# State updates cut into 64x64 products, and three moves in the order of a chunked retention prologue

## The chip, the cores and the metric

The kernel runs on one core of a Trainium2 chip. The core has TensorE (PE, with its weight loads shown apart as PEld), VectorE (DVE), ScalarE (ACT) and GpSimd (POOL), each with its own instruction stream, and SyncE (SP), whose queue issues the DMAs here. The metric is device microseconds of one execution, as the median over runs. A profiled execution has a span besides, from the first to the last instruction; its own time is a little longer than that.

## The reference, cut to what matters

Inputs are q, k and v of 4 batches, 8 heads, 768 positions and 64 columns, and three weight matrices of a bilinear FFN. The first part is a recurrence over the positions, the second a product over all 3072 tokens.

```python
gamma = 1.0 - 2.0 ** (-5.0 - np.arange(H))
for t in range(S):
    state = gamma * state + k[t] (outer) v[t]        # 64x64 for each batch and head
    y[:, :, t] = q[t] @ state / sqrt(64)
x = y, heads side by side                            # 3072 x 512
out = ((x @ w_a) * (x @ w_b)) @ w_out                # 512 -> 1536 -> 512
```

## The kernel before

Powers of gamma are folded into k and q when these are scaled, so the state is a plain running sum of k-by-v products. Positions are worked in slots of 128, two slots to a pair, and each slot in two chunks of 64 (c = 0 and 1). Within a chunk, a score matrix is formed (`scores`), masked to the causal part (`mask`), and multiplied by v (`intra`); what comes from earlier chunks is q times the state (`inter`). Both are summed in PSUM as y, and copied to xt, the FFN's input. The FFN makes a and g for 12 column blocks of 128 (`ffn_a`, `ffn_g`), multiplies them into ht, and forms the output rows (`ffn_out`).

The first batch, three pairs of slots (u = 0, 1, 2), has its own functions with a 2 in their names. For these a pair is loaded with even and odd positions apart (par = 0 and 1). For pairs 0 and 1:

- `casts2` (line 376) scales k and q and casts v, on DVE or POOL as the caller says; `scaled` is line 212, the casts are line 184.
- `flip2` (line 387) transposes k or q on TensorE (line 396) and copies the result out on ACT (line 182) as kT and qT.
- `scores2` (line 399) makes the scores of one parity (line 409) in PSUM, `mask2` (line 415) multiplies them by the mask on DVE (line 420), in two halves of rows.
- `update2` (line 423) adds a chunk's k-by-v products to the state in the PSUM tile st (line 432): for each parity and each of four head pairs one matmul with a contraction of 64 positions, 128 columns of k as weights and 128 columns of v. The product is 128x128, of which the two 64x64 blocks on the diagonal are used. `keep_state` (line 439) copies those blocks, a half of the partitions each, into the bf16 tile gbd, of which there are two, one for each chunk.
- `intra2` (line 455, matmul at 465) and `inter2` (line 444, matmul at 450) make y; `inter2` reads gbd[0] for c = 0 and gbd[1] for c = 1. `leave2` (line 470) copies y to xt, one chunk on each of two engines.
- `warm` (line 485) runs matmuls on zeros whose result nobody reads.

The order on each engine is the order of the program: every instruction is tied to the one before it on its engine. So the list of calls from line 553 on is the order of the work, on TensorE, ACT, DVE, POOL and SP alike, and an engine does nothing else while its next instruction waits. State tile st is one buffer: an update waits for the copies of the state that still read it. The pool psff has three buffers, taken in turn by transposes, scores, a and g; y0, y1, at and st have one each.

The DMA loads are issued on SP in the order of `LOADS` (line 20): k, q of pair 0, k, q of pair 1, v of both, then weights; POOL casts the weights as they land (`cast_w`, line 186, and `cast_o`).

Of the kernel before, what the change touches and what calls it, by code (L numbers as in the profile page):

```python
# [9 lines left out]
F32 = mybir.dt.float32  # L10
# [13 lines left out]
def kernel(  # L24
# [39 lines left out]
    psat = ctx.enter_context(tc.tile_pool(name="psat", bufs=1, space=bass.MemoryType.PSUM))  # L64
    psst = ctx.enter_context(tc.tile_pool(name="psst", bufs=1, space=bass.MemoryType.PSUM))
# [110 lines left out]
    wa_bf = wpool.tile([P, KT, DFF], BF16, name="wa_bf")  # L176
# [3 lines left out]
    def cast(engine, dst, src):  # L180
        if engine is nc.scalar:
            seq(nc.scalar.copy(dst, src))  # L182
        else:
            seq(engine.tensor_copy(dst, src))  # L184
# [50 lines left out]
    def half(i):  # L235
        return slice(64 * i, 64 * i + 64)
# [178 lines left out]
    def mask2(u, par, rows=(0, 1)):  # L415
        t = 2 * u + par
        if t not in aT:
            aT[t] = tra.tile([P, 2, HP, P], BF16, tag="aT", name="aT")
        for r in rows:
            seq(nc.vector.tensor_tensor(aT[t][:, r], ats[t][r], masks[par].to_broadcast([P, HP, P]),  # L420
                                        op=ALU.mult))

    def update2(u, c, on=(nc.scalar, nc.scalar)):
        if (u, c) == (PAIRS - 1, 1):
            return
        if (u, c) == (0, 0):
            state[0] = psst.tile([P, HP, P], F32, tag="st", name="st")
        st = state[0]
        for par in range(2):
            for hp in range(HP):  # L430
                t = 2 * u + par
                seq(nc.tensor.matmul(st[:, hp, :], kb[t][half(c), hp, :, :],  # L432
                                     vb[t].rearrange("p (r hp) d -> p hp r d", r=2)[half(c), hp],
                                     start=((u, c, hp, par) == (0, 0, 0, 0)),
                                     stop=(hp == HP - 1), skip_group_check=True))
        if on:
            keep_state(c, on)

    def keep_state(c, on=(nc.scalar, nc.scalar)):

        for r in range(2):
            cast(on[r], gbd[1 - c][half(r), :, half(r)], state[0][half(r), :, half(r)])

    def inter2(u, last=False):
        for c in range(2):
# [9 lines left out]
    def intra2(u, par, begin, home=None):  # L455
        if begin and home is None:
            ys[u] = [psat.tile([P, HP, P], F32, tag=f"y{c}", name="y") for c in range(2)]
        elif begin:
            both = psat.tile([P, 2, HP, P], F32, tag=home, name="y")
            ys[u] = [both[:, c] for c in range(2)]  # L460
        t = 2 * u + par
        for r in range(2):
            for hp in range(HP):
                for c in range(2):
                    seq(nc.tensor.matmul(ys[u][c][half(hp % 2), 2 * r + hp // 2, :],  # L465
                                         vb[t][half(c), HP * r + hp, :], aT[t][half(c), r, hp, :],
                                         start=(begin and r == 0 and hp < 2), stop=not begin,
                                         skip_group_check=True))

    def leave2(u, on):  # L470
        J, i = where[2 * u]
        if i == 0 and J not in xt:
            xt[J] = xtp.tile([P, 4, KT, P], BF16, tag="xt", name="xt")
        for c, eng in enumerate(on):
            if eng is None:
                continue
            cast(eng, xt[J][:, i + c].rearrange("p k (m par) -> p k par m", par=2),
                 ys[u][c].rearrange("p k (par m) -> p k par m", par=2))

    def xcols(J, kt, c0, c1):  # L480
        if J < 2:
            return xt[J][:, c0 // P : c1 // P, kt, :]
        return xt[J][:, kt, c0:c1]

    def warm(n, pool, tag, w=2 * P):
        idle = pool.tile([P, 4 * P], F32, tag=tag, name="idle")
        for _ in range(n):
            seq(nc.tensor.matmul(idle[:, :w], zero[:, :P], zero[:, :w], start=True, stop=True,  # L488
                                 skip_group_check=True))
# [2 lines left out]

    asbs = {}

    def ffn_a(J, ft, c0=0, c1=None):
        c1 = TILES[J] * P if c1 is None else c1
        if J not in ht:
            ht[J] = htp.tile([P, NFT, 4 * P], BF16, tag="ht", name="ht")
        fs = slice(ft * P, (ft + 1) * P)
        a = psff.tile([P, 4 * P], F32, tag="ff", name="a")[:, : c1 - c0]  # L500
        for kt in range(KT):
            seq(nc.tensor.matmul(a, wa_bf[:, kt, fs], xcols(J, kt, c0, c1),  # L502
                                 start=(kt == 0), stop=(kt == KT - 1)))
        asb = asbs[J, ft, c0] = asbp.tile([P, 4 * P], BF16, tag="asb", name="asb")[:, : c1 - c0]
        seq(nc.scalar.copy(asb, a))  # L505

    def ffn_g(J, ft, c0=0, c1=None):
        c1 = TILES[J] * P if c1 is None else c1
        fs = slice(ft * P, (ft + 1) * P)
        g = psff.tile([P, 4 * P], F32, tag="ff", name="g")[:, : c1 - c0]  # L510
        for kt in range(KT):
            seq(nc.tensor.matmul(g, wb_bf[:, kt, fs], xcols(J, kt, c0, c1),  # L512
                                 start=(kt == 0), stop=(kt == KT - 1)))
        seq(nc.vector.tensor_tensor(ht[J][:, ft, c0:c1], g, asbs.pop((J, ft, c0)), op=ALU.mult))  # L514

    def ffn_ab(J, ft):
# [40 lines left out]
    casts2(1, {(V, 0): G_, (V, 1): G_})  # L557
    cast_w(0, 2)
    flip2(0, K, [((0,), A_), ((1,), A_)])
    warm(8, psat, "y1", 64)  # L560
    flip2(0, Q, [((0,), A_)])
    warm(2, psat, "y1", P)
    flip2(0, Q, [((1,), A_)])
    warm(4, psat, "y1", 192)
    scores2(0, 0)
    scores2(0, 1, True)
    mask2(0, 0, (0,))
    casts2(1, {(Q, 1): D_})
    mask2(0, 0, (1,))
    mask2(0, 1)  # L570
    flip2(1, K, [((0, 1), A_)])
    warm(3, psst, "st", 4 * P)
    flip2(1, Q, [((1,), A_), ((0,), A_)], ("y0", "y1"))
    warm(3, psst, "st", 4 * P)
    scores2(1, 0)
    update2(0, 0)
    mask2(1, 0)
    intra2(0, 0, True)
    scores2(1, 1, True)
    mask2(1, 1)  # L580
    intra2(0, 1, False)
    leave2(0, (A_, None))
    update2(0, 1)
    inter2(0, True)
    leave2(0, (None, D_))
    intra2(1, 0, True, "at")
    update2(1, 0, (A_, D_))
    intra2(1, 1, False)
    W2 = 2 * P
    ffn_a(0, 0, 0, W2)  # L590
    inter2(1, True)
    leave2(1, (A_, D_))
    ffn_a(0, 1, 0, W2)
    update2(1, 1, None)
    issue_loads(100)
# [105 lines left out]
```

## Time and profile before

| what | value |
|---|---|
| median of 3 runs | 226.9 us (226.57 to 227.45) |
| the profiled execution's own time | 227.3 us |
| its span | 225.6 us |
| TensorE busy | 217.3 us, 2556 matmuls |
| DVE, ACT, POOL busy | 97.0, 96.3, 79.7 us |
| from HBM, to HBM | 28.31 MB, 6.29 MB |

Lines of the profile that show a group give its line in the kernel, engine, operation, the tiles written and read, shapes, and the count. In the timeline the first two numbers are the start and the length in us, from the first start to the last end of a merged group; a matmul's end lies about 0.2 us behind its start even for a narrow one, since matmuls are pipelined, so what a group takes of TensorE is read from the start of one group to the start of the next. In square brackets stands the idle time of the engine before the group and what ended it. The chain lists start, length and what the end was waiting for at that time. PEld is the weight loads, which run beside PE.

### The profile page before, as it was taken

To read this page: it belongs to the slowest core of one execution; us is meant where nothing else is said; L and a number is where in the kernel's file an instruction comes from. 1 tells how busy PE (TensorE), PEld (TensorE's weight loads), DVE (VectorE), ACT (ScalarE), POOL (GpSimd) and SP (SyncE) were. 2 spreads that over 40 slices of the span, in tenths; PEclk is the share of its full clock that TensorE was granted. 3 is DMA by queue.
4 is the path that set the end of the run, shared out by engine and by line. 5 is a ranking of instruction groups with operands and counts; after the bars stand their busy time and mean duration, and the time that the engine had idled before them with its cause. 6 is when DMAs were issued, how large, how long until landed. Compare 5 with 4: busy or idle time off the path is not lost.

```text
span 225.6 us, 6154 instructions
## 1 busy us (share of the span) xinstructions
PE 217.3 (96%) x2556; PEld 130.9 (58%) x2576; DVE 97.0 (43%) x196; ACT 96.3 (43%) x207; POOL 79.7 (35%) x104
## 2 busy tenths in 40 slices
PE   7799999999999999999999999999999999999994
PEld 7567445686446867875875444545444544444443
DVE  3885246643506435562466243445243422333300
ACT  3555424342427426455457433355433354333221
POOL 5467798783636151453534262350000000000000
PEclk9999999999999999999999999999999999999999
DMA  6999999999999996979899797858100012100022
GB/s 176 347 379 382 367 293 397 310 198 223 241 222 269 241 212 128 254 148 243 169 213 167 177 275 145 196 96 142 46 0 3 0 49 96 46 0 1 3 93 94
DMA packets 96124, 39.72 MB, mean 176 GB/s; under 512 B 76000, under 2 KB 91616, under 8 KB 96096
## 3 DMA queue, kind: packets, MB, share of 16 engines
q1 hardware_dynamic: 95952, 39.20, 69.4%
q8 instruction: 20, 0.33, 0.6%
q10 hardware_dynamic: 144, 0.13, 0.2%
q14 instruction: 8, 0.07, 0.1%
HBM read 28.31 MB, written 6.29 MB: 153 GB/s over the span
## 4 chain that ended last, share of the span: by engine, by line
PE 92%; DMA 2%; ACT 2%; issue 1%; DVE 1%; SPq 0%; DVEq 0%
PE a L502 28%; PE g L512 28%; PE o L539 27%; DMA qf<-in_q_dram 2%; PE y L321 2%; PE at L280 1%; PE y L333 1%; PE st L257 1%; ACT qT L182 1%; PE st L432 1%; PE tp L396 1%; DVE kqb L212 1%; PE at L409 1%; PE y L465 1%; PE y L450 1%
## 5 line engine op out<-in xcount | busy, mean ns | idle before, releaser
L514 DVE TENSOR_TENSOR ht<-g,asb 128x256 bf16<-128x256 f32 (+1 forms) x98 | 53.9, 550 | 84.0 <-PE g L512 72.8
L512 PE MATMUL g<-xt,wb_bf 128*128 128x256 bf16 (+1 forms) x389 | 77.5, 322 | 0.2
L502 PE MATMUL a<-xt,wa_bf 128*128 128x256 bf16 (+1 forms) x389 | 77.3, 322 | 0.1
L505 ACT CAST asb<-a 128x256 bf16<-128x256 f32 (+1 forms) x98 | 46.3, 472 | 71.7 <-PE a L502 70.5
L539 PE MATMUL o<-wo_bf,ht 128*128 128x512 bf16 (+2 forms) x299 | 62.5, 362 | 1.4 <-issue 1.1
L502 PEld LDWEIGHTS <-wa_bf 128*128 128x128 bf16 x392 | 38.0, 98 | 25.0 <-DVE xt L184 0.4
L512 PEld LDWEIGHTS <-wb_bf 128*128 128x128 bf16 x392 | 38.1, 98 | 23.8
L539 PEld LDWEIGHTS <-ht 128*128 128x128 bf16 x312 | 28.8, 98 | 30.6
L212 POOL TENSOR_TENSOR kqb<-kf,ktab 128x512 bf16<-128x512 f32 x21 | 22.3, 1062 | 41.6 <-DMA kf<-in_k_dram 41.6
L182 ACT COPY osb<-o 128x512 f32<-128x512 f32 (+2 forms) x25 | 14.1, 564 | 33.4 <-PE o L539 24.2
L212 POOL TENSOR_TENSOR kqb<-qf,qtab 128x512 bf16<-128x512 f32 x21 | 21.8, 1042 | 0.9 <-DMA qf<-in_q_dram 0.7
L184 POOL CAST vb<-vf 128x512 bf16<-128x512 f32 x25 | 15.0, 612 | 19.9 <-DMA vf<-in_v_dram 10.9
L182 ACT CAST gst<-sums 128x256 bf16<-128x256 f32 x33 | 13.4, 405 | 6.1 <-DVE sums L271 2.8
L271 DVE TENSOR_TENSOR sums<-st,sums 128x256 f32<-128x256 f32 x30 | 12.7, 424 | 1.7
L286 DVE TENSOR_TENSOR aT<-at,mask 128x512 bf16<-128x512 f32 x18 | 11.5, 679 | 0.0
L344 ACT CAST xt<-y 128x512 bf16<-128x512 f32 x16 | 8.5, 583 | 0.0
L488 PE MATMUL idle<-zero 128*128 128x170 bf16 (+4 forms) x55 | 7.0, 291 | 1.3 <-DVE zero L126 1.3
L420 DVE TENSOR_TENSOR aT<-at,mask 128x512 bf16<-128x512 f32 x12 | 7.5, 680 | 1.1 <-PE at L409 1.1
L184 POOL CAST wa_bf<-wsta 128x1024 bf16<-128x1024 f32 (+1 forms) x7 | 6.4, 918 | 2.5 <-DMA wsta<-in_moe_w_a_dram 2.5
L184 POOL CAST wo_bf<-wsto 128x1024 bf16<-128x1024 f32 x6 | 6.2, 1040 | 2.2 <-DMA wsto<-in_moe_w_out_dram 2.2
L184 POOL CAST wb_bf<-wstb 128x1024 bf16<-128x1024 f32 (+1 forms) x7 | 6.4, 918 | 1.6 <-DMA wstb<-in_moe_w_b_dram 1.4
L298 DVE COPY lgr<-bq 128x1 f32<-128x1 f32 x4 | 0.6, 154 | 14.2 <-PE y L321 14.2
(54 smaller groups left out, 93.3 us busy)
## 6 DMA issues: line engine op xcount, KB each, us to landing
out_dram<-osb SPq DMA_DIRECT2D x23, 256.0 KB, 2.8
kf<-in_k_dram SPq DMA_DIRECT2D x18, 256.0 KB, 4.0
qf<-in_q_dram SPq DMA_DIRECT2D x18, 256.0 KB, 4.2
vf<-in_v_dram SPq DMA_DIRECT2D x18, 256.0 KB, 4.6
wsta<-in_moe_w_a_dram SPq DMA_DIRECT2D x6, 512.0 KB, 7.7
wstb<-in_moe_w_b_dram SPq DMA_DIRECT2D x6, 512.0 KB, 7.9
wsto<-in_moe_w_out_dram SPq DMA_DIRECT2D x6, 512.0 KB, 8.2
kf<-in_k_dram SPq DMA_DIRECT2D x3, 512.0 KB, 6.0
```

The costliest lines, as they stand in the source:

```text
L182: seq(nc.scalar.copy(dst, src))
L184: seq(engine.tensor_copy(dst, src))
L212: seq(eng.tensor_tensor(dst, src, tab, op=ALU.mult))
L271: seq(nc.vector.tensor_tensor(new, u[c][:, s], old, op=ALU.add))
L286: seq(nc.vector.tensor_tensor(aT[n][:, r].rearrange("p s h d -> p (s h) d"), at[:, r].rearrange("p s h d -> p (s h) d"), mask.to_broadcast ...
L344: seq(nc.scalar.copy(dst, ys[o][c]))
L420: seq(nc.vector.tensor_tensor(aT[t][:, r], ats[t][r], masks[par].to_broadcast([P, HP, P]), op=ALU.mult))
L502: seq(nc.tensor.matmul(a, wa_bf[:, kt, fs], xcols(J, kt, c0, c1), start=(kt == 0), stop=(kt == KT - 1)))
L505: seq(nc.scalar.copy(asb, a))
L512: seq(nc.tensor.matmul(g, wb_bf[:, kt, fs], xcols(J, kt, c0, c1), start=(kt == 0), stop=(kt == KT - 1)))
L514: seq(nc.vector.tensor_tensor(ht[J][:, ft, c0:c1], g, asbs.pop((J, ft, c0)), op=ALU.mult))
L539: seq(nc.tensor.matmul(o, ht[J][:, ft, i * P : (i + 1) * P], wo_bf[:, ft, c0:c1], start=(ft == 0), stop=(ft == NFT - 1)))
```

## The change

Four things change.

1. `update2` makes two matmuls in place of one: 64 columns of k and the 64 columns of v of the same head, so that only the two blocks that are used are computed. Each writes its own half of the partitions of st, which now has 64 columns per head pair instead of 128. An update has 16 matmuls and 16 weight loads, before 8 and 8. `keep_state` copies all columns of a half.
2. Order on TensorE: `update2(0, 0)` ahead of `scores2(1, 0)`, `update2(0, 1)` ahead of `intra2(0, 1)`, `update2(1, 0)` ahead of `intra2(1, 0)`, and `inter2(1)` ahead of the first `ffn_a`. With them ACT's order: the copies of the state after `update2(0, 1)` stand ahead of the copy of y to xt, and both copies after `update2(1, 0)` are on ACT, where one was on DVE.
3. Order on DVE: pair 1's second q scaling stands ahead of all masks, where it stood between the two halves of the first one.
4. Matmuls on zeros: 10 in place of 8 with 64 columns, 3 with 96 columns in place of 2 with 128, and 2 in place of 3 with 512 columns at two places. And the a and g products of column blocks 2 and 3 of the first FFN group are done in two halves of 256 columns instead of one of 512 (`parts`).

On POOL and SP the instructions and their order are the same.

```diff
@@ update2, keep_state
-            state[0] = psst.tile([P, HP, P], F32, tag="st", name="st")
+            state[0] = psst.tile([P, HP, D], F32, tag="st", name="st")
...
-                seq(nc.tensor.matmul(st[:, hp, :], kb[t][half(c), hp, :, :],
-                                     vb[t].rearrange("p (r hp) d -> p hp r d", r=2)[half(c), hp],
+                for r in range(2):
+                    t = 2 * u + par
+                    seq(nc.tensor.matmul(st[half(r), hp, :], kb[t][half(c), hp, r, :],
+                                         vb[t][half(c), HP * r + hp, :],
...
-            cast(on[r], gbd[1 - c][half(r), :, half(r)], state[0][half(r), :, half(r)])
+            cast(on[r], gbd[1 - c][half(r), :, half(r)], state[0][half(r), :, :])
@@ ffn_a (ffn_g alike)
+    def parts(J, ft, c0, c1):
+        if J == 0 and ft in (2, 3):
+            return [(c0, (c0 + c1) // 2), ((c0 + c1) // 2, c1)]
+        return [(c0, c1)]
...
-            seq(nc.tensor.matmul(a, wa_bf[:, kt, fs], xcols(J, kt, c0, c1),
-                                 start=(kt == 0), stop=(kt == KT - 1)))
+            for b0, b1 in parts(J, ft, c0, c1):
+                seq(nc.tensor.matmul(a[:, b0 - c0 : b1 - c0], wa_bf[:, kt, fs], xcols(J, kt, b0, b1),
+                                     start=(kt == 0 and b0 == c0), stop=(kt == KT - 1 and b1 == c1),
+                                     skip_group_check=True))
@@ the order
-    warm(8, psat, "y1", 64)
+    warm(10, psat, "y1", 64)
     flip2(0, Q, [((0,), A_)])
-    warm(2, psat, "y1", P)
+    warm(3, psat, "y1", 96)
     flip2(0, Q, [((1,), A_)])
     warm(4, psat, "y1", 192)
     scores2(0, 0)
     scores2(0, 1, True)
-    mask2(0, 0, (0,))
     casts2(1, {(Q, 1): D_})
-    mask2(0, 0, (1,))
+    mask2(0, 0)
     mask2(0, 1)
     flip2(1, K, [((0, 1), A_)])
-    warm(3, psst, "st", 4 * P)
+    warm(2, psst, "st", 4 * P)
     flip2(1, Q, [((1,), A_), ((0,), A_)], ("y0", "y1"))
-    warm(3, psst, "st", 4 * P)
+    warm(2, psst, "st", 4 * P)
+    update2(0, 0)
     scores2(1, 0)
-    update2(0, 0)
     mask2(1, 0)
     intra2(0, 0, True)
     scores2(1, 1, True)
     mask2(1, 1)
+    update2(0, 1)
     intra2(0, 1, False)
+    inter2(0, True)
     leave2(0, (A_, None))
-    update2(0, 1)
-    inter2(0, True)
     leave2(0, (None, D_))
+    update2(1, 0)
     intra2(1, 0, True, "at")
-    update2(1, 0, (A_, D_))
     intra2(1, 1, False)
+    inter2(1, True)
+    leave2(1, (A_, D_))
     W2 = 2 * P
     ffn_a(0, 0, 0, W2)
-    inter2(1, True)
-    leave2(1, (A_, D_))
     ffn_a(0, 1, 0, W2)
     update2(1, 1, None)
```

More of the change, by code (lines that the diff above doesn't have):

```diff
@@ L430, in update2 @@
             for hp in range(HP):
-                t = 2 * u + par
-                seq(nc.tensor.matmul(st[:, hp, :], kb[t][half(c), hp, :, :],
-                                     vb[t].rearrange("p (r hp) d -> p hp r d", r=2)[half(c), hp],
-                                     start=((u, c, hp, par) == (0, 0, 0, 0)),
-                                     stop=(hp == HP - 1), skip_group_check=True))
+                for r in range(2):
+                    t = 2 * u + par
+                    seq(nc.tensor.matmul(st[half(r), hp, :], kb[t][half(c), hp, r, :],
+                                         vb[t][half(c), HP * r + hp, :],
+                                         start=((u, c, hp, par) == (0, 0, 0, 0)),
+                                         stop=(hp == HP - 1), skip_group_check=True))
         if on:
@@ L511, in ffn_g @@
         for kt in range(KT):
-            seq(nc.tensor.matmul(g, wb_bf[:, kt, fs], xcols(J, kt, c0, c1),
-                                 start=(kt == 0), stop=(kt == KT - 1)))
+            for b0, b1 in parts(J, ft, c0, c1):
+                seq(nc.tensor.matmul(g[:, b0 - c0 : b1 - c0], wb_bf[:, kt, fs], xcols(J, kt, b0, b1),
+                                     start=(kt == 0 and b0 == c0), stop=(kt == KT - 1 and b1 == c1),
+                                     skip_group_check=True))
         seq(nc.vector.tensor_tensor(ht[J][:, ft, c0:c1], g, asbs.pop((J, ft, c0)), op=ALU.mult))
```

## The prediction

> **What bounds the kernel now.** I read the totals and the chain's shares first, then the stretches, then the chain and the rows of each engine between 7 and 20 us, where the diff acts.
>
> ```profile
> span 225.6 us, 6154 instructions
> PE 92%; DMA 2%; ACT 2%; issue 1%; DVE 1%; SPq 0%; DVEq 0%
> ```
> ```profile
> 10.00:15.00 5.00, 4.19 (x96) 2.85 (x95) 4.71 (x8) 3.21 (x6) 3.02 (x5) 1.00 1.11 368
> ...
> 20.00:25.00 5.00, 5.00 (x34) 3.15 (x33) 1.72 (x5) 2.54 (x6) 3.61 (x5) 1.00 1.09 384
> ```
>
> Columns of the stretches: length, busy time of PE, PEld, DVE, ACT and POOL, granted clock, DMA share, GB/s. TensorE carries 92% of the chain and from 20 us it is busy without a break, at a granted clock of 1.00. So a microsecond taken off the start of the first full FFN products is a microsecond off the end, as long as what they read has come by then. From 10 to 15 us DVE is busy 4.71 of 5.00 us, more than PE.
>
> ```profile
> 9.39 0.69 DVE aT L420
> 10.08 1.12 DVE kqb L212
> ...
> 11.68 1.08 ACT qT L182 x2
> ...
> 12.80 0.42 PE at L409 x16
> ...
> 14.61 0.74 ACT xt L182
> 15.36 0.27 ACT gbd L182
> ...
> 15.63 0.38 ACT gbd L182
> ...
> 16.05 0.60 PE st L432 x8
> ```
>
> This is the chain: pair 1's q scaling waits behind a mask on DVE, its transposes and copies wait for it, and scores of pair 1 begin at 12.80. Then PE runs, with one detour over ACT: the xt copy (0.74) stands ahead of two state copies that the next update waits for.
>
> **q scaled ahead of all masks.**
>
> ```profile
> 3.37 1.57 SPq L95 DMA_DIRECT2D qf<-in_q_dram  x1
> ```
> ```profile
> DMA to landing us min/median/max: 6.1/6.1/6.1
> ```
> ```profile
> 7.92 0.69 DVE L212 TENSOR_TENSOR kqb<-kf,ktab 128x512 bf16<-128x512 f32 x1
> 10.00 1.19 DVE L212 TENSOR_TENSOR kqb<-qf,qtab 128x512 bf16<-128x512 f32 x1
> ```
> ```profile
> 8.04 1.47 POOL L212 TENSOR_TENSOR kqb<-kf,ktab 128x512 bf16<-128x512 f32 x1 [3.81 <-DMA kf<-in_k_dram]
> 9.60 1.04 POOL L212 TENSOR_TENSOR kqb<-qf,qtab 128x512 bf16<-128x512 f32 x1
> 11.01 1.21 POOL L184 CAST vb<-vf 128x512 bf16<-128x512 f32 x2 [0.37 <-DMA vf<-in_v_dram]
> ```
>
> Pair 1's q lands at 3.37+6.1 = 9.47. DVE, free by then, would start its scaling at 9.5, just ahead of POOL's at 9.60. Two scalings at once hold each other up: at 7.92 DVE was first and took 0.69 while POOL's took 1.47; at 10.00 POOL was first and DVE's took 1.19. With DVE first it ends at 10.2 instead of 11.19, and POOL's moves from 10.64 to about 11.05, harmless to its v casts (11.01 to 12.22 become about 11.05 to 12.27). The price is on the masks: eight at 0.62 follow (rows below), from 10.1 on.
>
> ```profile
> 10.22 1.01 ACT L182 COPY kT<-tp 128x1024 bf16<-128x1024 bf16 x1 [1.35 <-PE tp L396]
> 13.81 0.76 ACT L182 CAST gbd<-st 64x256 bf16<-64x256 f32 x2 [1.05 <-PE st L432]
> ```
> ```profile
> 11.11 1.87 DVE L420 TENSOR_TENSOR aT<-at,mask 128x512 bf16<-128x512 f32 x3
> ```
>
> The 0.99 us is not all gained: ACT copies kT until 11.23, so the two qT copies (1.08 in the chain) run 11.26 to 12.33, not 11.68 to 12.76. What is late next is this kT copy: gain 0.43. Two of the six 128x512 warm products go, and the smaller warm runs ahead of them change from 8 to 10 and from 2x128 to 3x96 columns; all stand before a wait for a scaling or a copy, so I cost them at nothing; without that cover the three extra small products would cost under 0.15 us.
>
> **Updates as 64x64 products.**
>
> ```profile
> 12.80 0.42 PE L409 MATMUL at<-qT,kT 64*64 64x128 bf16 x16 [0.29 <-ACT qT L182]
> 13.15 0.62 PE L432 MATMUL st<-vb,kqb 64*128 64x128 bf16 x8
> 13.70 0.42 PE L465 MATMUL y<-aT,vb 64*64 64x128 bf16 x16
> 13.95 0.39 PE L409 MATMUL at<-qT,kT 64*64 64x128 bf16 x16
> 14.17 0.39 PE L465 MATMUL y<-aT,vb 64*64 64x128 bf16 x16
> ...
> 56.01 0.45 PE L257 MATMUL st<-vb,kqb 64*64 64x64 bf16 x32
> 56.28 0.49 PE L280 MATMUL at<-kqT 64*64 64x64 bf16 x32
> ```
>
> From start to start the old update takes 0.55, and the scores ahead of it 0.35, where the same scores followed by another 64x64 shape take 0.22: changing the shape costs some 0.1 on each side. The new form doubles the instructions to 16 weight loads and 16 matmuls of 64 columns. Line 257 has that very form: 32 in 0.27 us, spread over four quadrants, eight rounds. The new update uses two (one row half, both column halves), so 16 of them are eight rounds too: 0.27. Bounds: 0.27 if loads hide, 0.55 if nothing is won, and above that if they don't hide (a rival below). I take 0.27, the row of the same form.
>
> The Trainium skill, "TensorE: Matmul & The Clock Gate", Part 3, The mechanism, says that a weight load overlaps matmuls in flight only where its row group differs; all 16 of an update share one. By it every load would be exposed and the change would lose. This trace speaks against it: line 432's eight share a row half and still start within 0.55.
>
> **The new order, forward from 12.3.** Update(0,0) waits only for pair 0's v cast (12.27), so half of it is done in the shadow of the qT copies, the rest by 12.46. Then scores 0.22 to 12.68, intra 0.22 to 12.90, scores to 13.12 (the masks of pair 0 are done by 10.1+4x0.62 = 12.6). Now the state copies bind. An update's result comes 0.45−0.27 = 0.18 after its last start; ACT starts 0.04 later, its two copies take 0.76, and the next update, which overwrites what they read, starts 0.05 later. Copies 12.68 to 13.44, update(0,1) 13.49 to 13.76; copies 13.98 to 14.74, update(1,0) 14.79 to 15.06, with intra and inter of pair 0 inside the wait. PE idles there about 0.35 and 0.4 us. The xt copy follows those copies now, 14.72 to 15.47, and so the third pair of copies runs 15.4 to 16.14; the second half of inter(1) starts at 16.19 and ends, switch included, at 16.51. Pair 1's masks end at about 15.4, just ahead of intra(1,1): DVE is almost as late as ACT, but not later. Both of pair 1's state copies are ACT's now, and in the old order the one on DVE waited for ACT's anyway.
>
> ```profile
> 18.05 0.61 PE L502 MATMUL a<-xt,wa_bf 128*128 128x256 bf16 x4
> 18.59 0.62 PE L432 MATMUL st<-vb,kqb 64*128 64x128 bf16 x8
> 19.14 0.61 PE L512 MATMUL g<-xt,wb_bf 128*128 128x256 bf16 x4
> 19.72 1.03 PE L502 MATMUL a<-xt,wa_bf 128*128 128x256 bf16 x8
> ```
>
> Behind inter(1) come a, a, update(1,1), g. With 0.54, 0.44 (no switch behind it but the update's 0.1), 0.37 with switches, and 0.5: 16.51+1.9 = 18.4 for the first product on pair 1's columns, against 19.72. Its xt copies, ACT then DVE at 0.74 each, end near 18.2, so they cover. Gain at this point: 1.3 us.
>
> **Behind it.** Update(2,0) stands in the part where TensorE has no break and saves 0.55−0.27 = 0.28 (0.3 with the shorter scores ahead). The a and g products of column blocks 2 and 3 are cut from 512 to 2x256: 16 more matmuls and loads.
>
> ```profile
> 21.90 1.89 PE L502 MATMUL a<-xt,wa_bf 128*128 128x512 bf16 x8
> 23.63 1.89 PE L512 MATMUL g<-xt,wb_bf 128*128 128x512 bf16 x8
> ...
> 44.59 0.60 PE L502 MATMUL a<-xt,wa_bf 128*128 128x256 bf16 x4
> 45.03 0.60 PE L512 MATMUL g<-xt,wb_bf 128*128 128x256 bf16 x4
> ```
>
> A 512 takes (23.63−21.90)/8 = 0.216, two 256 take 2x0.44/4 = 0.22: the cut costs 16x0.002 to 0.004, under 0.1 us. No DMA, SP or POOL instruction is moved.
>
> Does the gain last? Weights and pair 2 come at times that DMA and POOL set. The tightest that I found:
>
> ```profile
> 30.91 2.04 POOL L212 TENSOR_TENSOR kqb<-qf,qtab 128x512 bf16<-128x512 f32 x2
> ```
> ```profile
> 35.30 0.78 PE L396 MATMUL tp<-ident,kqb 128*128 128x128 bf16 x8
> ```
>
> Pair 2's q is scaled by 32.95 and its transposes run at 35.30; 1.3 earlier, at 34.0, they still find it, with 1.0 to spare. I take the whole 1.3 as kept. If DMA held them up, the gain would shrink only from 2.3 us on.
>
> **The sum.** The profiled execution took 227.3 us, its span 225.6 and 1.7 around it. 1.3 + 0.3 − 0.04 = 1.6 off: span 224.0, time 225.7. That execution lies 0.4 above the median of 226.9, so against the median I predict 226.9 − 1.6 = 225.3.
>
> **Rivals.**
> 1. The narrow loads do not hide (slower). Place: all five updates, since their 16 loads share a row half.
> ```profile
> L257 PEld LDWEIGHTS <-kqb 64*64 64x64 bf16 x264 | 3.2, 109 | 0.4 <-issue 0.4
> ```
> A load of this form lasts 0.109. If each pair of quadrants pays it in turn, an update takes 0.27 + 8x0.109 = 1.14, which is 0.87 over my value: half of it on update(0,0), all of it on the other four, 3.9 us, so 226.9 − 1.6 + 3.9 = 229.2. It decides from where an update costs about 0.36 more than I take (1.6/4.5), 0.63 each. For it: no row of this trace has this form on one row half alone. Against it: line 257 hides loads that last as long, line 432 hides loads on one row half. 1 in 10. It is also what the skill's sentence on row groups would give.
> 2. The split products are no shorter (0.55 each), so the edit does not do what it says. Update(0,1) and (1,0) lose 0.28 each on the loop with ACT, (1,1) and (2,0) as much, (0,0) half of it: 1.3 of the 1.6 is gone, 226.6, no change. For it: twice the instructions. Against it: lines 257, 465 and 409 start theirs at 0.27 or less per 32 or 0.22 per 16. 15 in 100.
> 3. POOL takes the q scaling first, as at 10.00. Then DVE's ends at about 11.15, the qT copies at 12.7, and eight masks from 11.07 end at about 15.95; scores(1,1) wait for a mask until 13.6 and DVE sets the pace to intra(1,1). Inter(1) ends at 16.8, 0.3 later, gain 1.3, 225.6, still faster by 0.57%. For it: the two start within 0.1 us. Against: at 7.92 DVE was first by 0.12 from one landing that both waited for. 15 in 100.
> 4. Waits on ACT longer than 0.05 each, or pair 2's data late after all: gain 0.5 to 1.0, about 226.1, within 0.5%. 7 in 100.
>
> **How the numbers follow.** The forecast as it stands has 53 in 100, with its own range of 224.8 to 225.8 (each of the three ACT waits and the update known to some 0.1 to 0.15). 0.5%, 1.1 us, is about what a measurement of this kernel can tell from no change: the line is at 225.8. Faster: 53 plus 13 of case 3, 0.66. Same: cases 2 and 4 and the rest of 3, 0.24. Slower: 0.10. The range of 224.7 to 226.9 takes in cases 2 to 4 and leaves out the slower one and some above and below.
>
> **What would show it.** Scores of pair 1 starting at 12.4 to 12.5, with update(0,0) ahead of them (at 12.80 before); DVE's third scaling at 9.5 lasting 0.69 and POOL's second one over 1.3; each update 16 matmuls in 0.27 from start to start; two PE waits of 0.3 to 0.4 us ended by the state copies, and one in the middle of inter(1); the first product on pair 1's columns near 18.4 (19.72 before); the first product on column block 2 some 1.3 earlier than 21.90; pair 2's transposes not waiting for POOL. The prediction is wrong if an update takes over 0.5, if a mask rather than a state copy ends PE's waits, if the cut 2x256 products take more than two 512s' share, or if the 1.3 is handed back at a wait between 20 and 45 us.

## The result, and the profile after

The changed kernel takes 225.6 us (median of 5 runs, 225.39 to 226.01), the kernel before 226.97 (5 runs, 226.57 to 227.45). The ratio is 0.9941, with a 95% interval of 0.9921 to 0.996: 1.37 us less, 0.59%. The profiled execution took 225.51, its span 223.8.

The page of the changed kernel, its span and the shares of its chain:

```profile
span 223.8 us, 6287 instructions
...
PE 93%; DMA 3%; POOL 1%; ACT 1%; SPq 0%; issue 0%; DVE 0%; POOLq 0%
```

DVE's share of the chain has gone from 1% to 0% and ACT's from 2% to 1%, and POOL stands in it for 1%. The chain between 9 and 24 us of the changed kernel (start, length, what was waited for) tells why:

```profile
9.52 1.49 POOL kqb L212
...
11.06 0.40 PE tp L396 x4
11.45 0.45 PE idle L488 x2
...
11.94 0.55 PE st L433 x16
...
12.52 0.37 ACT gbd L182
...
12.91 0.38 ACT gbd L182
...
13.33 0.35 PE st L433 x11
```

POOL's half of pair 1's q is now the last to be scaled (9.52 to 11.01), where DVE's was. Behind it come transposes, zero products, the first update, and then twice the two state copies on ACT and the update that waits for them. TensorE's timeline of the changed kernel, in the same columns as before the change:

```profile
11.94 0.54 PE L433 MATMUL st<-vb,kqb 64*64 64x64 bf16 x16
12.29 0.42 PE L409 MATMUL at<-qT,kT 64*64 64x128 bf16 x16
12.52 0.42 PE L465 MATMUL y<-aT,vb 64*64 64x128 bf16 x16
...
13.33 0.35 PE L433 MATMUL st<-vb,kqb 64*64 64x64 bf16 x11 [0.17 <-ACT gbd L182]
13.48 0.25 PE L465 MATMUL y<-aT,vb 64*64 64x128 bf16 x2
13.51 0.23 PE L433 MATMUL st<-vb,kqb 64*64 64x64 bf16 x4
13.56 0.22 PE L465 MATMUL y<-aT,vb 64*64 64x128 bf16 x2
13.57 0.19 PE L433 MATMUL st<-vb,kqb 64*64 64x64 bf16 x1
...
14.60 0.38 PE L433 MATMUL st<-vb,kqb 64*64 64x64 bf16 x12 [0.20 <-ACT gbd L182]
...
16.21 1.05 PE L509 MATMUL a<-xt,wa_bf 128*128 128x256 bf16 x8
17.19 0.44 PE L433 MATMUL st<-vb,kqb 64*64 64x64 bf16 x16
17.56 0.61 PE L521 MATMUL g<-xt,wb_bf 128*128 128x256 bf16 x4
18.01 1.04 PE L509 MATMUL a<-xt,wa_bf 128*128 128x256 bf16 x8
...
20.19 1.91 PE L509 MATMUL a<-xt,wa_bf 128*128 128x256 bf16 x16
```

The scores of pair 1 start at 12.29 (12.80 before), the first product on pair 1's columns at 18.01 (19.72), the first on column block 2 at 20.19 (21.90). The 16 products of update(0,1) start between 13.33 and 13.57, and the next group runs on at 13.58, so they take 0.25 us; the 8 old ones of this update took 0.53 (14.62 to 15.15).

To compare runs I cut each profiled execution at places that all kernels have: the first scores of pair 0, the first product on pair 1's columns (called the mark from here on), the first and the last FFN output product, and the end of the span. "Mark 9.74" is short for 9.74 us from the first scores to the mark.

| stretch, us | before | changed | gain |
|---|---|---|---|
| start to first scores of pair 0 | 8.92 | 8.85 | 0.07 |
| to the mark | 10.80 | 9.16 | 1.64 |
| to the first output product | 33.60 | 33.43 | 0.17 |
| to the last output product | 168.92 | 168.68 | 0.24 |
| to the end of the span | 3.35 | 3.67 | −0.32 |
| span | 225.59 | 223.79 | 1.80 |

By the last output product 2.1 us have been gained, at the end 1.8. Something is given back, and not only in the last row. Near 112 us, in a stretch that the change does not touch, the changed kernel has a new wait; the rows are TensorE's, then DVE's:

```profile
111.66 0.60 PE L521 MATMUL g<-xt,wb_bf 128*128 128x256 bf16 x4
112.34 0.60 PE L509 MATMUL a<-xt,wa_bf 128*128 128x256 bf16 x4
```
```profile
110.62 0.42 DVE L524 TENSOR_TENSOR ht<-g,asb 128x256 bf16<-128x256 f32 x1 [0.45 <-PE g L521]
111.87 0.92 DVE L524 TENSOR_TENSOR ht<-g,asb 128x256 bf16<-128x256 f32 x2 [0.83 <-PE a L509]
```

Groups of four products follow each other at 0.44 all through this stage; here one takes 0.68. The ht product that should have run at about 111.49 starts at 111.87 and ends at 112.29, and TensorE's next a starts 0.05 later. In the trace DVE's wait for its operands had ended at 111.44. So 0.25 us goes on a DVE instruction that starts late although all it needs is there. And the last store takes longer to land. The rows are the DMA issues after 216 us, of the changed kernel and of the kernel before; the last number is us to landing:

```profile
out_dram<-osb SPq DMA_DIRECT2D x1, 128.0 KB, 2.0
```
```profile
out_dram<-osb SPq DMA_DIRECT2D x1, 128.0 KB, 1.7
```

These two, 0.25 and 0.32, are more than a quarter of what was gained ahead of them: 0.07 + 1.64 + 0.17 = 1.88, less 0.57 is 1.31, next to the 1.37 of the medians. (The 0.07 ahead of the first scores is not the change's: in the kernels below, e9_one_more_dve apart, these scores start anywhere from 8.71 to 8.99.) The profiled executions differ by 0.4 to 0.5 more because the stretch around 116 to 126 us took 10.08 before and 9.67 after; over all runs below but e9_one_more_dve it took 9.66 to 10.22 and followed no edit, so I don't count it.

### The profile page after: what moved, and what is told of

The parts are those of the page before. It is cut to its first block, busy times and chain, and to the rows that moved or that the text cites. A ratio compares the mean times of both kernels' runs of the same rounds, so it can differ in the third digit from the quotient of the medians.

```text
span 223.8 us, 6287 instructions
## 1 busy us (share of the span) xinstructions
PE 217.3 (97%) x2633; PEld 131.6 (59%) x2633; DVE 96.2 (43%) x195; ACT 96.6 (43%) x208; POOL 79.9 (36%) x104
## 3 DMA queue, kind: packets, MB, share of 16 engines
q1 hardware_dynamic: 95952, 39.20, 67.2%
## 4 chain that ended last, share of the span: by engine, by line
PE 93%; DMA 3%; POOL 1%; ACT 1%; SPq 0%; issue 0%; DVE 0%; POOLq 0%
PE o L549 28%; PE a L509 28%; PE g L521 28%; DMA kf<-in_k_dram 3%; PE y L321 1%; POOL kqb L212 1%; PE at L280 1%; PE y L333 1%; PE st L257 1%; PE st L433 1%; ACT gbd L182 1%; PE tp L396 1%; PE y L450 1%; PE y L465 1%; SPq L95 0%
## 5 line engine op out<-in xcount | busy, mean ns | idle before, releaser
L549 PE MATMUL o<-wo_bf,ht 128*128 128x512 bf16 (+2 forms) x312 | 64.4, 363 | 0.0
L509 PEld LDWEIGHTS <-wa_bf 128*128 128x128 bf16 x400 | 38.9, 98 | 24.2 <-issue 0.5
L521 PEld LDWEIGHTS <-wb_bf 128*128 128x128 bf16 x400 | 38.9, 98 | 22.9
L212 POOL TENSOR_TENSOR kqb<-qf,qtab 128x512 bf16<-128x512 f32 x21 | 22.3, 1066 | 1.1 <-DMA qf<-in_q_dram 1.0
```

What stands on the lines that cost most here:

```text
L212: seq(eng.tensor_tensor(dst, src, tab, op=ALU.mult))
L509: seq(nc.tensor.matmul(a[:, b0 - c0 : b1 - c0], wa_bf[:, kt, fs], xcols(J, kt, b0, b1), start=(kt == 0 and b0 == c0), stop=(kt == KT - 1 a ...
L521: seq(nc.tensor.matmul(g[:, b0 - c0 : b1 - c0], wb_bf[:, kt, fs], xcols(J, kt, b0, b1), start=(kt == 0 and b0 == c0), stop=(kt == KT - 1 a ...
L549: seq(nc.tensor.matmul(o, ht[J][:, ft, i * P : (i + 1) * P], wo_bf[:, ft, c0:c1], start=(ft == 0), stop=(ft == NFT - 1)))
```

## The experiments

"Before" is the kernel before, which ran beside each of them on the same chip. Ratios are to it, with a 95% interval, from 5 rounds.

### Which part of the change brings what

**e1_wide_update**: the changed kernel with the old products in the update, and with them the old state tile of 128 columns per head pair and its copies.

```diff
-                for r in range(2):
-                    t = 2 * u + par
-                    seq(nc.tensor.matmul(st[half(r), hp, :], kb[t][half(c), hp, r, :],
-                                         vb[t][half(c), HP * r + hp, :],
...
+                t = 2 * u + par
+                seq(nc.tensor.matmul(st[:, hp, :], kb[t][half(c), hp, :, :],
+                                     vb[t].rearrange("p (r hp) d -> p hp r d", r=2)[half(c), hp],
...
```

> The changed kernel with the old update (8 products of 128 columns, state tile of 128). Mark: start of the first product on pair 1's columns (19.72 before, 18.01 after). My theory: in the new order the pace is set by the loop of update, state copies on ACT and next update, so each update on it adds only its longer run (0.25 to 0.5, switches included) partly beside copies: mark near 18.5, update(2,0) 0.2 more, total 0.7 over the changed kernel, 226.3 us. Rival (the work counts in full, five times 0.28 and the switches): 1.4 to 1.9 over it, 227.0 to 227.5. Rival (the narrow products are no shorter): the same as the changed kernel, 225.6.

Measured: 226.81 us (226.29 to 227.46), ratio 0.9985 (0.9972 to 0.9998). Mark 9.74, 0.58 more than the changed kernel, and from the mark to the first output product 33.65, 0.22 more. So the narrow update is worth 0.80 in the trace, and 1.0 by the ratios. TensorE's rows of this kernel:

```profile
13.49 0.60 PE L432 MATMUL st<-vb,kqb 64*128 64x128 bf16 x8
14.02 0.42 PE L465 MATMUL y<-aT,vb 64*64 64x128 bf16 x16
```

0.53 from the update to what follows it, 0.25 in the changed kernel (13.33 to 13.58).

**e2_narrow_alone**: the kernel before with only this part changed (the same lines the other way round).

> The kernel before with the narrow update alone, all in the old order. My theory: update(0,0), (1,0), (1,1) and (2,0) become 0.3 shorter each on TensorE, but ACT's xt copy ahead of the state copies and DVE's xt copy hold part of it back: mark near 19.07 (0.65 earlier than 19.72), total 0.85 under before, 226.1 us. Rival (work counts in full): 1.4 to 1.9 under, 225.1 to 225.6, and then the order was worth nothing.

Measured: 226.34 us (226.1 to 226.94), ratio 0.9969 (0.9956 to 0.9981). The mark comes 0.52 sooner after the first scores (10.28), the first output product another 0.2. In the old order, too, the narrow products gain; they need no help of the new one.

**e3_q_alone**: the kernel before with only the q scaling ahead of all masks.

```diff
-    mask2(0, 0, (0,))
     casts2(1, {(Q, 1): D_})
-    mask2(0, 0, (1,))
+    mask2(0, 0)
```

> The kernel before with pair 1's second q scaling ahead of all masks, nothing else. My theory: DVE's scaling takes 0.69 from about 9.5, the kT copy holds the qT copies, scores of pair 1 start 0.44 earlier (12.36), and all of it arrives at the mark (19.28) and the end: 226.5 us. Rival (the masks, now later, take the place of the wait): scores earlier, mark unmoved, 226.9 us.

Measured: 226.64 us (226.27 to 227.25), ratio 0.9981 (0.9968 to 0.9993). Mark 10.32 after the first scores, 0.48 sooner.

**e4_mask_first**: the changed kernel with DVE's old order (the same three lines the other way round).

> The changed kernel with the old order on DVE (half of the first mask, then the q scaling, then the rest). My theory: the qT copies end 0.6 later (12.76), but update(0,0) is then wholly done beside them; the first state copies can't start before ACT is free, 0.25 later than 12.52; mark 0.25 later (18.26), total 225.85 us. Rival (the whole 0.4 to 0.6 comes back): 226.1 us. Rival (DVE's masks bind, which end no later in this order): 225.6 us.

Measured: 226.13 us (225.9 to 226.82), ratio 0.9957 (0.994 to 0.9974). Mark 9.49, 0.33 later than in the changed kernel, and 0.36 us more by the ratios. The intervals of the two ratios overlap, so it is the mark that shows the step and not the time.

**e5_no_cut**: the changed kernel with 512 columns at once in blocks 2 and 3.

```diff
-        if J == 0 and ft in (2, 3):
+        if False:
```

> The changed kernel without the cut of column blocks 2 and 3 into 2x256. My theory: the cut cost 0.04 us on TensorE and did nothing else: 225.55 us, no difference that can be measured; from the first product on block 2 to the one on block 4 3.45 us in place of 3.49. Rival (the cut keeps TensorE fed where a 512 would wait for a weight cast or a buffer): 0.2 to 0.5 slower and a wait in that stretch.

Measured: 225.85 us (225.62 to 226.0), ratio 0.9939 (0.9924 to 0.9955), not to be told from the changed kernel's 0.9941. From the mark to the first output product 33.39, 0.04 less: the price that was predicted.

**e6_old_order**: the kernel before with the narrow update and the q scaling ahead, in the old order of calls and with its zero products (e2 and e3 together).

> The kernel before with the narrow update and the q scaling ahead of the masks, but the old order on TensorE and ACT, the old warm products and no cut. My theory: mark near 18.6, 1.3 under before, 225.7 us, so the new order is worth about 0.5. Rival (the order is worth nothing once the other two are there): mark at 18.0 and 225.2 to 225.6 us. Rival (state copies behind the xt copy cost their whole 0.74): mark near 18.8, 225.9 us.

Measured: 225.89 us (225.77 to 226.45), ratio 0.9946 (0.9931 to 0.9962). Mark 9.79: 1.01 sooner than before, just the sum of 0.52 and 0.48. The new order of calls and the zero products, which the changed kernel has on top, bring 0.63 more at the mark (9.16) and next to nothing in the time (0.9941, where the intervals leave room for about half a us either way). What they bring is given back: this kernel has neither the wait at 112 us nor the slow last store (1.70). DVE's rows of this kernel at the same place:

```profile
111.19 0.43 DVE L514 TENSOR_TENSOR ht<-g,asb 128x256 bf16<-128x256 f32 x1 [0.45 <-PE g L512]
112.08 0.42 DVE L514 TENSOR_TENSOR ht<-g,asb 128x256 bf16<-128x256 f32 x1 [0.46 <-PE g L512]
```

**e7_old_warms**: the changed kernel with the old counts of zero products.

```diff
-    warm(10, psat, "y1", 64)
+    warm(8, psat, "y1", 64)
...
-    warm(3, psat, "y1", 96)
+    warm(2, psat, "y1", P)
...
-    warm(2, psst, "st", 4 * P)
+    warm(3, psst, "st", 4 * P)
...
-    warm(2, psst, "st", 4 * P)
+    warm(3, psst, "st", 4 * P)
```

> The changed kernel with the old counts of products on zeros. The prediction costed them at nothing. From the changed kernel's chain, which runs through two of them just ahead of update(0,0), I expect now: the third product of the first 512 block hidden by POOL's scaling, the third of the second block 0.2 on the path, mark 0.2 later (18.2), 225.8 us. Rival (hidden by the v cast and the qT copies): mark at 18.0, 225.6 us.

Measured: 226.28 us (225.77 to 226.53), ratio 0.9958 (0.9941 to 0.9974). Mark 9.29, 0.13 later than in the changed kernel: update(0,0) stands behind the third zero product. By the ratios it is 0.39 slower, with intervals that overlap, and the rest of that is not in the stretch that the edit touches; its profiled execution lost 0.55 in the stretch around 120 us that varies by itself.

**e8_delay**: the changed kernel with five more 128x512 zero products ahead of column block 2, to see if TensorE's time there is the kernel's time. They add work and leave out none.

```diff
+    warm(5, psat, "y1", 4 * P)
```

> The changed kernel with five more 128x512 products on zeros (1.08 us by 0.216 each) behind the last product of the first two column blocks. My theory: TensorE is the bound from there to the end, so all of it arrives: 1.1 over the changed kernel, 226.7 us. Rival (weights, pair 2 or the tail wait for DMA and give part of the gain back anyway): less than 0.6 over it, under 226.2 us.

Measured: 227.27 us (226.77 to 227.8), ratio 1.0005 (0.9992 to 1.0018). TensorE's rows of this kernel:

```profile
20.41 1.24 PE L488 MATMUL idle<-zero 128*128 128x512 bf16 x5
21.49 0.71 PE L509 MATMUL a<-xt,wa_bf 128*128 128x256 bf16 x5
```

1.08 is put in, 1.08 is found at the first output product (34.51 from the mark instead of 33.43), and the time is 1.45 above the changed kernel's by the ratios. All of it arrives: no transfer downstream was waiting to take the gain. The 0.37 above what was put in I can't place; this kernel's profiled execution took 7.84 and 10.18 in the two turns between stages where the changed kernel's took 7.49 and 9.67, which vary in other runs too.

### What is given back

The profiles of all these kernels showed the wait near 112 us in some and not in others, and it went with the count of entries that the trace has on DVE: 322 where it occurs, 323 where not. In the first, the 192nd entry of DVE's record is an ht product; it starts about 0.4 us after its wait has ended. In the others the 192nd entry is the wait itself, which would have waited anyway. (The expectation of e9_one_more_dve counts one entry fewer.) The slow last store went, up to here, with both counts: ACT has 340 entries where DVE has 322, and 339 where DVE has 323.

**e11_before_moved**: the kernel before, with one of two copies of pair 2's q moved from DVE to ACT, so that both lists get the counts of the changed kernel. If place is the cause, the kernel before gets both delays.

```diff
-    flip2(2, Q, [((0,), D_), ((1,), D_)], ("y1", "y0"))
+    flip2(2, Q, [((0,), D_), ((1,), A_)], ("y1", "y0"))
```

> The kernel before with one of the two copies of pair 2's q at 36 us on ACT instead of DVE, nothing else. Theory (place in the stream): from there on DVE has one fewer and ACT one more, so the stall of 0.25 near 114 us and the 2.0 us of the last store appear in the old order too: 0.5 to 0.6 slower than before, 227.5 us. Rival (times or the new order): neither appears, 226.9 to 227.0 us.

Measured: 227.44 us (227.26 to 228.14), ratio 1.0022 (1.0011 to 1.0032), last store 2.11. TensorE's rows of this kernel:

```profile
113.44 0.60 PE L512 MATMUL g<-xt,wb_bf 128*128 128x256 bf16 x4
114.13 0.60 PE L502 MATMUL a<-xt,wa_bf 128*128 128x256 bf16 x4
```

Both delays are there, without any part of the change, and cost 0.5 us.

**e10_copy_back**: the changed kernel with one of the copies that `keep_state(1)` makes behind update(1,1) on DVE again (the call on its own, off the chain).

```diff
-    keep_state(1)
+    keep_state(1, (A_, D_))
```

> The changed kernel with one of the two state copies after update(1,1), far off the path at 19.4 us, on DVE instead of ACT, so that from there on both engines have as many instructions ahead as in the kernel before. Theory (place in the stream): stall at 112 us gone and the last store back at 1.7: 0.25 + 0.33 less, 225.05 us. Theory that only DVE's count matters for the stall and ACT's for the store: the same here. Rival (times or the order): both stay, 225.6 us.

Measured: 225.5 us (225.13 to 225.92), ratio 0.9932 (0.9919 to 0.9945). The last store lands in 1.70 again. The wait of 0.25 stays: the list grew by two entries (the copy and a wait of its own, 324), and the 192nd is again an ht product, that of one block earlier. DVE's rows of this kernel show the late start moved with it (the timeline's products at 0.87 apart, then 1.25):

```profile
109.87 0.42 DVE L524 TENSOR_TENSOR ht<-g,asb 128x256 bf16<-128x256 f32 x1 [0.45 <-PE g L521]
111.12 0.93 DVE L524 TENSOR_TENSOR ht<-g,asb 128x256 bf16<-128x256 f32 x2 [0.82 <-PE a L509]
```

That is what a place would do, and what a certain block's work would not. The median is the lowest of all, but the intervals of this kernel and the changed one overlap, so it is not shown to be faster.

**e9_one_more_dve**: the changed kernel with one more instruction on DVE, at its start, that fills a new tile of 4 bytes per partition which nobody reads.

```diff
+    spare = const.tile([P, 1], F32, name="spare")
+    seq(nc.vector.memset(spare, 0.0))
```

> The changed kernel with one more instruction on DVE, a memset of a column that nobody reads, at 1.3 us where DVE waits anyway. In all runs of the new order so far a DVE product of stage J=4 (its 191st instruction in the profile) starts 0.42 us after its semaphore and TensorE stalls 0.25 there, and the last store takes 2.0 us to land; in all runs of the old order neither is seen (1.7 us). Theory: what counts is how many instructions stand ahead on the engine; the new order has one fewer on DVE and one more on ACT, and at some places in the stream an engine gets its next instructions late. Then the stall at 112 us goes here, minus 0.25, 225.35 us, and the store stays at 2.0 unless it too hangs on DVE. Rival: stall and store follow from the earlier times or from the new order itself: both stay, 225.6 us.

Measured: 231.53 us (229.23 to 235.41), ratio 1.0152 (1.0113 to 1.0191). The wait near 112 us is gone, as the place would have it (323 entries; the first 22 groups of a and g of that stage take 9.61 instead of 9.86), but the kernel is 5 us slower than the changed one by the ratios, for another reason. The rows of its page: GB/s in 40 slices, and the packets of the loads' queue; behind them the same two of the changed kernel.

```profile
GB/s 171 290 329 348 342 283 365 356 220 136 221 242 215 266 185 144 135 215 151 224 146 167 213 174 236 186 213 152 103 0 0 0 39 75 71 3 1 0 90 91
...
q1 hardware_dynamic: 95952, 39.20, 76.7%
```
```profile
GB/s 177 347 379 382 366 319 389 305 213 170 253 239 269 254 208 91 267 191 220 180 211 194 147 270 177 220 86 142 47 0 0 3 50 94 47 3 1 0 94 95
...
q1 hardware_dynamic: 95952, 39.20, 67.2%
```

The same packets and bytes took 76.7% of 233.7 us instead of 67.2% of 223.8, that is 179 instead of 150 us of each of the 16 engines, from the first loads on. The first scores come at 9.32 instead of 8.85, and around 120 us TensorE waits 7 us longer than in the changed kernel. (The profiled execution took 235.41, the longest of its six, so 179 and 7 stand for the worst of them; the granted clock fell to 0.52 between 125 and 130 us, behind that wait. The shortest, 229.23, is still slower than every run of the changed kernel.) The runs of the kernel before on the same chip were as ever, 227.01.

**e12_bq_twice**: one more instruction on DVE without a new tile. An existing small fill is written twice.

```diff
     seq(nc.vector.memset(bq, math.log(1.0 / 8.0)))
+    seq(nc.vector.memset(bq, math.log(1.0 / 8.0)))
```

> The changed kernel with one more small DVE instruction near its start, as in e9_one_more_dve, but without a new tile: the fill of bq is written twice, with the same value. Two questions. First, the wait of 0.25 us on TensorE near 112 us of the changed kernel. Theory A (it belongs to a place in DVE's list of instructions, and one instruction more moves the ht product off that place): the wait is gone, the two first quarters of the stage J=4 take 9.61 us and not 9.85, and the time is 0.25 below the changed kernel's, about 225.35. Theory B (it belongs to the new order of the work): the wait stays and the time is the changed kernel's, 225.6. Second, the slow loads of e9_one_more_dve (231.5 us). If the additional instruction makes them, this kernel is as slow, 229 to 232; if it was the new 4-byte tile, loads run at their usual pace, with the first scores of pair 0 near 8.8 us and not 9.3. The last store should land some 2.0 us before the end's mark as in the changed kernel, if its delay goes with ACT's list, which is the same here, and near 1.7 if it goes with DVE's.

Measured: 225.91 us (225.53 to 226.2), ratio 0.9942 (0.9926 to 0.9958). Loads run at their usual pace (67.2% of the span again, first scores at 8.93): the slowness of e9_one_more_dve came with the new tile, not with one more fill. The wait at 112 us stays:

```profile
112.05 0.60 PE L522 MATMUL g<-xt,wb_bf 128*128 128x256 bf16 x4
112.73 0.60 PE L510 MATMUL a<-xt,wa_bf 128*128 128x256 bf16 x4
```

By its letter that is theory B. But the trace also shows that the list did not grow: the second fill took over a wait that had an entry of its own, and DVE has 322 entries as in the changed kernel, with the ht product again at the 192nd. So what the run was to change was not changed, and it says nothing on the place. The last store takes 2.14, with 322 entries on DVE and 340 on ACT, which does not tell the two counts apart either.

**The place and the last store, over all 14 traces.** The 192nd entry is not the only such place. The 320th entry of DVE's list, 128 further on, is late too wherever it is something other than a wait. DVE's rows of its last copy, of the changed kernel, where it is the 318th entry, and of e10_copy_back, where it is the 320th:

```profile
219.76 0.29 DVE L184 COPY osb<-o 128x128 f32<-128x128 f32 x1 [9.04 <-PE o L549]
```
```profile
220.38 0.29 DVE L184 COPY osb<-o 128x128 f32<-128x128 f32 x1 [9.40 <-PE o L549]
```

The copy comes 0.36 later behind the work before it. In the five kernels with 323 entries the 320th is the instruction behind this copy, and starts 0.40 behind the copy's start instead of 0.04. (The 64th shows no such delay: in the changed kernel it is a mask that starts at once.)

e9_one_more_dve, with 323 entries on DVE and 340 on ACT, landed its last store in 1.82, so ACT's count is out, and DVE's is left: 1.69 to 1.86 in the six kernels with 323 or 324 entries, 2.02 to 2.26 in the eight with 322. One more thing goes with it in all 14 traces, a transfer of 8 KB on an instruction queue. In the six it starts 0.14 to 0.18 us behind the store's issue, always 0.66 to 0.69 behind the 320th entry's start, and is over by 0.54 to 0.86. In the eight, where the 320th entry is a wait that the engine comes to behind the copy, it starts at 0.56 to 0.58 and ends at 1.02 to 1.16, while the store's own packets run from 0.83 on. So the slow stores run beside this transfer for 0.19 us or more, the others for 0.03 at most. That it makes them slow is argued from the times; no run moved the transfer alone.

## Why the prediction was right, point by point

**The time.** 225.3 was predicted and 225.6 came, within the range, and faster by 0.59% where over 0.5% was given 0.66. That it came so close is in part luck, for two errors of opposite sign met in the sum: the gain at the mark was larger than predicted (1.64 for 1.3), what follows it up to the first output product was near what was predicted (0.17 for 0.26), and 0.57 that no term of the sum stands for was lost behind it.

**q scaled ahead of all masks: right.** The rows of the changed kernel, DVE's and then POOL's:

```profile
9.41 0.69 DVE L212 TENSOR_TENSOR kqb<-qf,qtab 128x512 bf16<-128x512 f32 x1 [0.87 <-DMA qf<-in_q_dram]
```
```profile
9.52 1.48 POOL L212 TENSOR_TENSOR kqb<-qf,qtab 128x512 bf16<-128x512 f32 x1
```

DVE was first, took 0.69, and POOL's was lengthened to 1.48 and ended at 11.00 (11.05 predicted); the third rival, POOL first, did not occur. What was late next was both that POOL scaling and the kT copy: the qT copies ran from 11.06, not 11.26 (the kT copy began 0.07 sooner, and a copy starts up to 0.1 ahead of the recorded end of the one before), and the scores at 12.29 instead of 12.4 to 12.5. Update(0,0) was over by then, as POOL's v casts ended at 12.12 and not at 12.27. Alone the step is worth 0.48 at the mark (e3_q_alone), 0.43 predicted.

**The update in 0.27: right, and a little less.** 16 products start within 0.24 to 0.25. The first and second rivals (loads that don't hide; products that are no shorter) are out. The sentence of the Trainium skill, "TensorE: Matmul & The Clock Gate", Part 3, The mechanism, that a load overlaps only where the row group differs, does not hold here: all 16 loads of update(0,1) are on one row half, and their products start 0.015 apart, while a load of this form took 0.109 in the profile of before. For update(2,0) the term was 0.3; the scores and the update took 36.87 to 38.00 before and 35.20 to 36.12 now, 1.13 and 0.92, so 0.21.

**State copies bind: right.** TensorE's two waits are ended by the gbd copies (0.17 and 0.20 in brackets, behind the drain of the group before); no mask ends one. The third wait, in the middle of inter(1), is down to about 0.08: two of its products start at 15.84 and 15.98, right behind a copy that ends at 15.93, where neighbouring pairs start 0.05 to 0.08 apart. ACT's rows of the changed kernel:

```profile
12.52 0.76 ACT L182 CAST gbd<-st 64x256 bf16<-64x256 f32 x2 [0.38 <-PE st L433]
13.80 0.74 ACT L182 CAST gbd<-st 64x256 bf16<-64x256 f32 x2 [0.53 <-PE st L433]
14.57 0.74 ACT L182 CAST xt<-y 128x512 bf16<-128x512 f32 x1
15.18 0.75 ACT L182 CAST gbd<-st 64x256 bf16<-64x256 f32 x2
```

The copies start at 12.52, 13.80 and 15.18 where 12.68, 13.98 and 15.4 were predicted: the 0.16 by which they began sooner, kept. Pair 2's transposes follow without a wait for POOL, as was said.

**The mark: mis-sized.** The step ran from 12.3 to 18.4, a gain of 1.3; the mark came at 18.01, a gain of 1.71 in this trace, 1.64 counted from the first scores. Of the 0.39 between 18.4 and 18.01, 0.30 stood at the end of inter(1) (16.21 for 16.51), and the four groups behind it took 1.80 for 1.9. The term that failed is the zero products, "I cost them at nothing": with the old counts update(0,0) waits behind a third one, 0.13 at the mark (e7_old_warms). 0.07 is the earlier start of this execution, and the remaining 0.2 is made of the small differences named above, which no run takes apart.

**The cut: right**, 0.04 (e5_no_cut).

**"I take the whole 1.3 as kept": wrong as to the tail.** No transfer took the gain, as e8_delay confirms; that far the reason was right. But two delays that belong to no row that I had read came in, 0.25 at a DVE instruction near 112 us and 0.32 at the last store. The signs that I had named looked only between 20 and 45 us. The runs tie the first to the place of an instruction in DVE's list: it occurs in the nine kernels whose 192nd entry is an ht product and in none of the five where it is a wait, in the old order as in the new, and it moves to another block's product when the list grows by two. A second place, the 320th, is late in the same way. That the cause is the supply of instructions at these places is only argued: the traces have two transfers on an instruction queue that start 0.1 to 1.9 us behind the 192nd entry, but they have them there in kernels without the delay too. The Trainium skill, "Runtime: NRT & Kernel Launch", Instruction fetch mechanics, tells of refills of an engine's instruction memory in blocks and holds their cost to be mostly hidden; no run here shows which engine's refill this is. The last store is slow in the eight kernels with 322 entries on DVE and in none of the six with more, beside an instruction transfer that runs at the same time; that this transfer is the cause is argued, not shown.

Put together, in gains at the mark: q scaling 0.48 and narrow update 0.52, each alone in the old order, and zero products 0.13, taken from the changed kernel. The order of calls was not run alone; what is left for it of the 1.64 is 0.5. The parts depend on each other: taken out of the changed kernel, q scaling costs 0.33 at the mark and the narrow update 0.58.

## What to carry to other kernels

Where one engine is busy to the end, read the gain at a mark close behind the edit, aligned to an event ahead of it, and then walk to the end stretch by stretch: the same change can be worth 1.8 us where it acts and 1.4 at the end. Moving an instruction from one engine's list to another shifts all that stands behind it in both, and may put a fixed delay onto a product on the chain or take it off; compare the far stages before crediting or blaming the edit. Products of which only diagonal blocks are used are worth cutting where many small products start faster than few wide ones: 16 of 64x64 took 0.25 us here, 8 of 64x128 took 0.53 to 0.55.

## What the hardware showed that I had not expected

- Products of two groups start out of program order. All 16 products of update(0,1) stand ahead of intra(0,1) in the program, but the rows above show four intra products started at 13.48 and 13.56, before the last update product at 13.57. The intra products use the two row halves of the array in turn, and the update's only one, so those that go ahead may be the ones on the other 64 rows; the rows do not say which they are. The Trainium skill, "TensorE: Matmul & The Clock Gate", Part 3, The mechanism, says that matmuls keep program order in start and end; by their starts, these don't. What it saves, no run shows.
- A DVE instruction at a fixed place of the list, the 192nd entry, started about 0.4 us late after its operands had come, in each of nine kernels; TensorE lost 0.25. The 320th entry was 0.36 late in each of six.
- The last store of 128 KB took 1.69 to 1.86 or 2.02 to 2.26 us to land in kernels that store the same data in the same way, the longer time where an 8 KB instruction transfer ran beside its packets.
- With a new tile of 4 bytes per partition at the start of the program all loads were slower (179 instead of 150 us of packet time for the same bytes, in the one execution profiled). A second fill of an existing tile did not do that. That the shift of all later tiles by 4 bytes is the cause is a guess that no run tested.
